# Attention weights turned by VectorE and a DRAM buffer, with a new order of units and a constant FFN pace

## The chip, the cores and the metric

The kernel runs on one core of one Trainium2 chip. The metric is the device time of one execution in microseconds (us); a quoted time is the median of a kernel's runs. In the profile of the kernel before, TensorE does the matrix products (9120 instructions), VectorE, ScalarE and GpSimd the other arithmetic (1650, 1185 and 1047), and SyncE issues the transfers (DMA) but for those of the output. "Clock" is the share of full speed that was granted to TensorE; in the 26 records of the trace before it is either 1 or one half.

## The reference

Attention with a threshold, on 8 batches of 8 heads (576 rows, head dimension 64), then a bilinear FFN over all 4608 rows. The three FFN weights come as float64 and are converted in the kernel.

```python
def _attn_ref(q, k, v, tau):                      # q, k, v: (8, 8, 576, 64)
    scale = 1.0 / np.sqrt(q.shape[-1])
    scores = scale * np.matmul(q, k.transpose(0, 1, 3, 2))
    thresh = np.max(scores, axis=-1, keepdims=True) - tau
    scores = np.where(scores >= thresh, scores, -1000000000.0)
    scores = scores - np.max(scores, axis=-1, keepdims=True)
    attn = np.exp(scores)
    attn = attn / (np.sum(attn, axis=-1, keepdims=True) + 1e-09)
    return np.matmul(attn, v).astype(np.float32)

def _moe_ref(x, w_a, w_b, w_out):                 # 512 -> 1536 -> 512
    return ((x @ w_a) * (x @ w_b) @ w_out).astype(np.float32)
```

## The kernel before

Two heads form a **pair**; there are 32. A pair has five **units**: four of 128 rows for each of its two heads (u = 0 to 3), and one with the last 64 rows of both (u = 4, the tail). A unit's scores go into two PSUM tiles (`sc`, two buffers), so the next unit's scores can start only when VectorE's mask has read these. Two units give a **half** (256 rows). Once the four pairs of a batch have delivered the same half, a block of 256 rows of FFN input `x` is complete.

```python
    def scores(i, u):
        ...
        sc = [ps_sc.tile([P, S], FP32, tag="sc", name="sc") for _ in range(n)]   # ps_sc: 2 buffers
        for c0, c1 in ((0, MAIN), (MAIN, S)):          # 512 columns, then 64
            for j in range(n):                         # the two heads: rows 0-63 and 64-127 of qT and kT
                ...
                    nc.tensor.matmul(sc[j][:, c0:c1], qT[r, u * P:(u + 1) * P],
                                     kT[r, c0:c1], start=True, stop=True)
        ...                                            # row maxima on VectorE, bias and threshold on GpSimd

    def weigh(i, u):
        ...
            nc.scalar.activation(w, s, AF.Exp, bias=bias[:, j:j + 1], scale=e_scale[:, 0:1])
        ...
            nc.vector.scalar_tensor_tensor(            # the mask; last reader of the PSUM tile
                out=ws[j], in0=s, scalar=thr[:, j:j + 1], in1=ws[j],
                op0=ALU.is_ge, op1=ALU.mult, accum_out=sums[:, j:j + 1])
        ...
        for j, w in enumerate(ws):
            nc.gpsimd.tensor_scalar(w, w, rcp[:, j:j + 1], None, op0=ALU.mult)
        weights[i, u] = ws

    def turn_pe(i, u):                                 # the weights must be turned for the product with v
        ...
                for s in range(4):
                    c = TAIL * j + s * P
                    nc.tensor.transpose(tp[:, s, :], w[:, c:c + P], ident)
                nc.scalar.copy(view[:, 5 * j:5 * j + 4], tp.rearrange("p s (i e) -> p s i e", e=Q))
        ...
```

FFN matmuls are strewn between the units: `advance(cols)` emits so many columns of them, at a `rate` set anew for each batch from what is waiting.

```python
    units = [(i, u) for i in range(NPR) for u in range(NT + 1)]
    ...
    for g in range(len(units) + PV_LAG):               # PV_LAG = 1
        if g < len(units):
            ...
            scores(i, u)
            ...
        if before is not None:
            turn(*before)                              # the unit before this one
        ...
            weigh(i, u)
            for _ in range(2):
                convert_weights()                      # float64 -> float32, a piece at a time
                load_weights(1)
        ...
        advance(rate)
        for what in due(g):
            weighted(*what)                            # product with v of a finished half
            if what[1] == 1 and what[0] % HP == HP - 1:
                rate = backlog() / (2 * UB)
        advance(rate)
```

## Time and profile before

| | before |
|---|---|
| time, median (lowest to highest of 4 runs) | 1920.09 us (1918.99 to 1921.74) |
| TensorE busy / mean clock | 1799.5 us of 1917.2 / 0.959 |
| VectorE, ScalarE, GpSimd busy | 711.5, 559.0, 808.2 us |

The page's picture of the span in 40 slices of 48 us gives the busy share of an engine in tenths (9 is 90% or more), and the granted clock likewise.

```profile
PE   4665868999999999999999999999999999999999
...
PEclk9666789999999999999999999999999999999999
```

TensorE is idle for more than a third of the first six slices and slowed in five of them, then full. The table of waits (who waited for what: us in total, times, longest) says what holds it there:

```profile
PE tp L287 <- POOL w L262: 51.1, 33, 4.3
PE sc L229 <- DVE w L255: 30.9, 9, 5.8
```

The largest wait is a turn that waits for GpSimd's scaling of the weights. The second, only nine times, is a score tile that waits for VectorE's mask to free a PSUM slot.

### The profile page before, as it was taken

What the parts mean: (1) busy time and instruction counts of PE and PEld (TensorE: products, weight loads), DVE (VectorE), ACT (ScalarE), POOL (GpSimd) and SP (SyncE); (2) the same over time, 40 slices, a digit from 0 to 9 for tenths busy, and PEclk for the clock granted to TensorE, in tenths of its full rate; (3) what the DMA queues carried; (4) which work ended last, traced back from release to release, by engine and by line L of the source; (5) the groups of instructions that cost most, each with busy time, mean ns of one, the idle gap of its engine ahead of it and who ended that gap; (6) DMA issues with size and microseconds to landing.
All of it is one profiled execution on the core that took longest, in us unless ns stands there. A gap on an engine that the chain in (4) does not pass through costs nothing.

```text
span 1917.2 us, 24375 instructions
## 1 busy us (share of the span) xinstructions
PE 1799.5 (94%) x9120; PEld 1219.7 (64%) x9120; DVE 711.5 (37%) x1650; ACT 559.0 (29%) x1185; POOL 808.2 (42%) x1047
## 2 busy tenths in 40 slices
PE   4665868999999999999999999999999999999999
PEld 2333545676757575757576767676757575758766
DVE  4666565343334333434333332332334333331000
ACT  2333322333333332333332222222323332331000
POOL 5788777434444344444444323323444344440000
PEclk9666789999999999999999999999999999999999
DMA  4223232111110111111111011001110100000000
GB/s 106 65 64 89 74 96 58 30 19 30 19 30 15 28 20 30 20 30 20 22 21 25 19 25 18 24 13 30 20 30 17 27 13 18 1 12 1 11 11 11
DMA packets 201157, 58.20 MB, mean 30 GB/s; under 512 B 191824, under 2 KB 191824, under 8 KB 201040
## 3 DMA queue, kind: packets, MB, share of 16 engines
q1 hardware_dynamic: 195792, 47.21, 11.6%
q10 hardware_dynamic: 5248, 9.44, 1.4%
q8 instruction: 72, 1.18, 0.2%
q14 instruction: 45, 0.37, 0.1%
HBM read 47.19 MB, written 9.44 MB: 30 GB/s over the span
## 4 chain that ended last, share of the span: by engine, by line
PE 84%; POOL 9%; DVE 4%; issue 2%; ACT 1%; SPq 0%; DMA 0%; POOLq 0%; DVEq 0%; ACTq 0%
PE pab L388 39%; PE po L404 20%; PE sc L229 7%; PE pv L358 6%; PE tp L287 6%; POOL w L262 4%; PE tp L293 2%; POOL low L170 2%; POOL low L169 2%; PE sc L232 2%; PE pv L355 1%; DVE w L255 1%; POOL bias L240 1%; POOL top L162 1%; DVE mx L239 1%
## 5 line engine op out<-in xcount | busy, mean ns | idle before, releaser
L262 POOL TENSOR_SCALAR w<-w,rcp 128x576 f32<-128x576 f32 x288 | 505.9, 1767 | 360.0 <-DVE rcp L260 354.0
L239 DVE TENSOR_REDUCE mx<-sc 128x1 f32<-128x576 f32 x288 | 207.3, 752 | 528.4 <-PE sc L229 458.2
L388 PE MATMUL pab<-xT,wb_sb 128*128 128x256 f32 x1536 | 389.8, 389 | 4.5 <-ACT wT L288 3.2
L404 PE MATMUL po<-wo_sb,h 128*128 128x512 f32 x864 | 389.5, 599 | 0.0
L388 PE MATMUL pab<-xT,wa_sb 128*128 128x256 f32 x1536 | 380.0, 387 | 7.2 <-ACT wT L294 7.2
L388 PEld LDWEIGHTS pab<-xT,wa_sb 128*128 128x128 f32 x1536 | 288.4, 191 | 66.0 <-issue 21.0
L388 PEld LDWEIGHTS pab<-xT,wb_sb 128*128 128x128 f32 x1536 | 287.6, 192 | 55.9 <-issue 10.5
L240 POOL TENSOR_SCALAR bias<-mx,e_nscale 128x1 f32<-128x1 f32 x288 | 95.2, 331 | 472.0 <-DVE mx L239 298.2
L255 DVE SCALAR_TENSOR_TENSOR w<-sc,thr,w 128x576 f32<-128x576 f32 x288 | 226.7, 815 | 142.0 <-ACT w L252 137.9
L404 PEld LDWEIGHTS po<-wo_sb,h 128*128 128x128 f32 x864 | 159.3, 190 | 184.0 <-issue 183.0
L288 ACT COPY wT<-tp 128x512 f32<-128x512 f32 x256 | 138.9, 588 | 415.6 <-PE tp L287 409.0
L252 ACT ACTIVATE w<-sc,bias,e_scale 128x576 f32<-128x576 f32 x288 | 230.3, 846 | 72.8 <-POOL bias L240 72.0
L398 DVE TENSOR_TENSOR h<-a,pab 128x256 f32<-128x256 f32 x216 | 90.6, 420 | 405.7 <-PE pab L388 405.3
L229 PE MATMUL sc<-kT,qT 64*128 64x512 f32 (+1 forms) x1024 | 200.8, 474 | 39.1 <-DVE w L255 30.9
L229 PEld LDWEIGHTS sc<-kT,qT 64*128 64x128 f32 x1024 | 105.9, 198 | 163.6 <-issue 153.3
L287 PE MATMUL tp<-ident,w 128*128 128x128 f32 x1024 | 152.5, 291 | 51.2 <-POOL w L262 51.1
L395 ACT COPY a<-pab 128x256 f32<-128x256 f32 x216 | 80.7, 374 | 364.0 <-PE pab L388 363.9
L287 PEld LDWEIGHTS tp<-ident,w 128*128 128x128 f32 x1024 | 116.9, 148 | 67.1 <-POOL w L262 61.3
L358 PE MATMUL pv<-wT,vm 128*64 128x256 f32 x1024 | 132.7, 404 | 0.0
L358 PEld LDWEIGHTS pv<-wT,vm 128*64 128x64 f32 x1024 | 71.3, 144 | 54.6 <-issue 29.2
L241 POOL TENSOR_SCALAR thr<-mx,cut 128x1 f32<-128x1 f32 x288 | 85.8, 298 | 0.0
L363 ACT COPY xT<-pv 128x256 f32<-128x256 f32 x64 | 23.8, 372 | 199.1 <-PE pv L358 186.6
(55 smaller groups left out, 990.4 us busy)
## 6 DMA issues: line engine op xcount, KB each, us to landing
qm<-in_q_dram SPq DMA_DIRECT2D x128, 72.0 KB, 2.4
km<-in_k_dram SPq DMA_DIRECT2D x128, 72.0 KB, 2.5
vm<-in_v_dram SPq DMA_DIRECT2D x64, 128.0 KB, 2.5
out_dram<-osb ACTq DMA_DIRECT2D x32, 256.0 KB, 2.0
raw<-in_moe_w_a_dram SPq DMA_DIRECT2D x12, 512.0 KB, 3.8
raw<-in_moe_w_b_dram SPq DMA_DIRECT2D x12, 512.0 KB, 3.8
raw<-in_moe_w_out_dram SPq DMA_DIRECT2D x12, 512.0 KB, 3.7
v_diag<-in_v_dram SPq DMA_DIRECT2D x64, 16.0 KB, 2.0
```

What stands on the lines that cost most here:

```text
L229: nc.tensor.matmul(sc[j][:, c0:c1], qT[r, u * P:(u + 1) * P], kT[r, c0:c1], start=True, stop=True)
L239: nc.vector.tensor_reduce(mx[:, c], sc[j], axis=AX.X, op=ALU.max)
L240: nc.gpsimd.tensor_scalar(bias[:, c], mx[:, c], e_nscale[:, 0:1], None, op0=ALU.mult)
L252: nc.scalar.activation(w, s, AF.Exp, bias=bias[:, j:j + 1], scale=e_scale[:, 0:1])
L255: nc.vector.scalar_tensor_tensor(out=ws[j], in0=s, scalar=thr[:, j:j + 1], in1=ws[j], op0=ALU.is_ge, op1=ALU.mult, accum_out=sums[:, j:j + 1])
L262: nc.gpsimd.tensor_scalar(w, w, rcp[:, j:j + 1], None, op0=ALU.mult)
L287: nc.tensor.transpose(tp[:, s, :], w[:, c:c + P], ident)
L288: nc.scalar.copy(view[:, 5 * j:5 * j + 4], tp.rearrange("p s (i e) -> p s i e", e=Q))
L358: nc.tensor.matmul(pv[j * D:(j + 1) * D], vm[:, j, s, :], wT[:, 5 * j + s, :], start=False, stop=(s == 3))
L388: nc.tensor.matmul(p, w[:, c, fs], xT[:, c, :], start=(c == 0), stop=(c == HP - 1))
L398: nc.vector.tensor_tensor(hid, a, pab[1], op=ALU.mult)
L404: nc.tensor.matmul(po, hs[F][:, u * P:(u + 1) * P], wo_sb[:, F, :], start=(F == 0), stop=(F == NF - 1))
```

## The change

The intent is to take the turns off TensorE, which is the bound. The kernel has VectorE turn the weights in blocks of 32x32 (256 turns of 128x576); the blocks themselves are then put in the partitions that the product with v reads by four stores to a DRAM buffer and one load of it. The product with v comes two units after a half's last unit instead of one. GpSimd gives the scaling of the weights to ScalarE, and the conversion of the FFN weights needs fewer operations. Units run in a new order, the first halves of four pairs and then their rest, so that the first FFN block is complete after 8 units. FFN runs at a constant pace. The diff, cut to its core:

```diff
-PV_LAG = 1
-WT_BUFS = 3
+PV_LAG = 2
+WT_BUFS = 2
+FFN_PACE = 0.09
...
+    scratch = pool("scratch", 3, space=bass.MemoryType.DRAM)
...                                        # convert_weights
-        nc.scalar.activation(low, lo, AF.Copy, bias=0.0, scale=2.0 ** -52)
-        nc.vector.tensor_scalar(top_u, hi, 0x7FFFFFFF, None, op0=ALU.bitwise_and)
+        nc.scalar.activation(top, hi.bitcast(FP32), AF.Abs)
+        nc.scalar.activation(low, lo, AF.Copy, bias=2.0 ** 23, scale=2.0 ** -29)
...
-        nc.gpsimd.tensor_tensor(low, low, t, op=ALU.mult)
-        nc.gpsimd.tensor_tensor(low, low, top, op=ALU.add)
...
+        nc.gpsimd.tensor_tensor(dst.bitcast(U32), top_u, low_u, op=ALU.add)
...                                        # turn
         for j, w in enumerate(ws):
-            nc.gpsimd.tensor_scalar(w, w, rcp[:, j:j + 1], None, op0=ALU.mult)
+            nc.scalar.activation(w, w, AF.Copy, scale=rcp[:, j:j + 1])
...                                        # turn_pe is gone; the VectorE turn of w into tb was there, unused
+            swap = scratch.tile([2 * NB, Q, G, W], FP32, tag="swap", name="swap")
+            for g in range(G):
+                nc.sync.dma_start(swap[:, :, g, :].rearrange("c p w -> p c w"),
+                                  tb[g * Q:(g + 1) * Q])
+            wT = work.tile([P, NSLOT, n], FP32, tag="wT", bufs=WT_BUFS, name="wT")
...
+        nc.sync.dma_start(wT, swap.rearrange("(s r) p g w -> (r p) s (g w)", r=G))
...
-    units = [(i, u) for i in range(NPR) for u in range(NT + 1)]
+    units = []
+    for i in range(0, NPR, HP):
+        units += [(p, u) for p in range(i, i + HP) for u in (0, 1)]
+        units += [(p, u) for p in range(i, i + HP) for u in (2, 3, 4)]
...
+                if g == max(first[p] - 4, 0):
+                    load_pair(p)
...
-        advance(rate)
+        advance(0.85 * PACE)
         for what in due(g):
             weighted(*what)
-            if what[1] == 1 and what[0] % HP == HP - 1:
-                rate = backlog() / (2 * UB)
-        advance(rate)
+        advance(0.15 * PACE)
```

More of the change, by code (lines that the diff above doesn't have):

```diff
@@ L20, in float_of @@
     return struct.unpack("<f", struct.pack("<I", bits))[0]
-DMA_FROM = 32
-PV_LAG = 1
-WT_BUFS = 3
+PV_LAG = 2
 XT_BUFS = 4
 W_BUFS = 4
+WT_BUFS = 2
+H_BUFS = 13
+FFN_PACE = 0.09
 @with_exitstack
@@ L76 @@
     HALF = MAIN // 2
+    GT = HALF // TAIL
     NSLOT = 9
-    GT = HALF // TAIL
+    G = P // Q
     SCALE = 1.0 / math.sqrt(D)
@@ L96 @@
     loaded = {}
-    NVD = 3
+    NVD = HP
     v_diag = [const.tile([P, 2, D], FP32, name=f"v_diag{i}") for i in range(NVD)]
@@ L110, in load_pair @@
             tiles[name] = t
-        vm = loads.tile([P, 2, NT, D], FP32, tag="vm", bufs=3, name="vm")
+        vm = loads.tile([P, 2, NT, D], FP32, tag="vm", bufs=HP, name="vm")
         vd = v_diag[i % NVD]
@@ L156, in convert_weights @@
         top = work.tile([P, CW], FP32, tag="osb", bufs=4, name="top")
-        t = work.tile([P, CW], FP32, tag="osb", bufs=4, name="t")
         low = work.tile([P, CW], FP32, tag="osb", bufs=4, name="low")
-        top_u, t_u = top.bitcast(U32), t.bitcast(U32)
-        nc.scalar.activation(low, lo, AF.Copy, bias=0.0, scale=2.0 ** -52)
-        nc.vector.tensor_scalar(top_u, hi, 0x7FFFFFFF, None, op0=ALU.bitwise_and)
-        nc.gpsimd.tensor_scalar(top, top, float_of(0x47F00000), float_of(0x38000000),
+        top_u, low_u = top.bitcast(U32), low.bitcast(U32)
+        nc.scalar.activation(top, hi.bitcast(FP32), AF.Abs)
+        nc.scalar.activation(low, lo, AF.Copy, bias=2.0 ** 23, scale=2.0 ** -29)
+        nc.gpsimd.tensor_scalar(top, top, float_of(0x47EFFFFF), float_of(0x38000000),
                                 op0=ALU.min, op1=ALU.max)
-        nc.vector.tensor_scalar(t_u, top_u, 3, 0x3FFFFFFF,
+        nc.scalar.activation(low_u, low, AF.Copy, bias=-(2.0 ** 23), scale=1.0)
+        nc.vector.tensor_scalar(top_u, top_u, 3, 0x3FFFFFFF,
                                 op0=ALU.logical_shift_left, op1=ALU.bitwise_and)
-        nc.vector.scalar_tensor_tensor(out=top_u, in0=top_u, scalar=0x40000000, in1=t_u,
+        nc.vector.scalar_tensor_tensor(out=top_u, in0=hi, scalar=0xC0000000, in1=top_u,
                                        op0=ALU.bitwise_and, op1=ALU.bitwise_or)
-        nc.vector.tensor_scalar(t_u, top_u, 0x7F800000, None, op0=ALU.bitwise_and)
-        nc.gpsimd.tensor_tensor(low, low, t, op=ALU.mult)
-        nc.gpsimd.tensor_tensor(low, low, top, op=ALU.add)
-        nc.vector.scalar_tensor_tensor(out=dst.bitcast(U32), in0=hi, scalar=0x80000000,
-                                       in1=low.bitcast(U32),
-                                       op0=ALU.bitwise_and, op1=ALU.bitwise_or)
+        nc.gpsimd.tensor_tensor(dst.bitcast(U32), top_u, low_u, op=ALU.add)
     for t in v_diag:
@@ L181 @@
     load_weights(2)
-    ident = const.tile([P, P], FP32, name="ident")
-    make_identity(nc, ident)
-    q_diag = [const.tile([P, P], FP32, name=f"q_diag{i}") for i in range(2)]
+    q_diag = [const.tile([P, P], FP32, name=f"q_diag{i}") for i in range(1)]
     for t in q_diag:
@@ L210, in prep, with prep_tail @@
         t = loaded[i]
-        qT = work.tile([P, S], FP32, tag="qT", name="qT")
-        kT = work.tile([P, S], FP32, tag="kT", name="kT")
+        qT = work.tile([P, S], FP32, tag="qT", bufs=HP, name="qT")
+        kT = work.tile([P, S], FP32, tag="kT", bufs=HP, name="kT")
         nc.vector.transpose(qT, t["q"].rearrange("p n e -> p (n e)"))
         nc.vector.transpose(kT, t["k"].rearrange("p n e -> p (n e)"))
-        qd = q_diag[i % 2]
+        prepared[i] = (qT, kT)
+    def prep_tail(i):
+        qT, qd = prepared[i][0], q_diag[0]
         for j in range(2):
@@ L218, in prep @@
             nc.gpsimd.tensor_copy(qd[r, j * TAIL:(j + 1) * TAIL], qT[r, MAIN:S])
-        prepared[i] = (qT, kT, qd)
     def scores(i, u):
-        qT, kT, qd = prepared[i]
+        qT, kT = prepared[i]
+        qd = q_diag[0]
         n = 2 if u < NT else 1
@@ L260, in weigh, with turn @@
         nc.vector.reciprocal(rcp[:, 0:n], sums[:, 0:n])
+        weights[i, u] = (ws, rcp)
+    def turn(i, u):
+        ws, rcp = weights.pop((i, u))
         for j, w in enumerate(ws):
-            nc.gpsimd.tensor_scalar(w, w, rcp[:, j:j + 1], None, op0=ALU.mult)
-        weights[i, u] = ws
-    def turned_tile(i, u):
-        h = u // 2
-        if (i, h) not in turned:
-            if u < NT:
-                turned[i, h] = work.tile([P, NSLOT, HALF], FP32, tag="wT", bufs=WT_BUFS, name="wT")
-            else:
-                turned[i, h] = work.tile([P, NSLOT, TAIL], FP32, tag="wTt", bufs=2, name="wTt")
-        return turned[i, h]
@@ L275, in turn_pe @@
-    def turn_pe(i, u):
-        ws = weights.pop((i, u))
-        wT = turned_tile(i, u)
-        if u < NT:
-            view = wT.rearrange("p s (i t e) -> p s i t e", i=4, e=Q)[:, :, :, u % 2, :]
-            tp = ps_1.tile([P, 4, P], FP32, tag="ps1", name="tp")
-            for j, w in enumerate(ws):
-                if j == 1:
-                    tp = ps_1.tile([P, 4, P], FP32, tag="ps1", name="tp")
-                for s in range(4):
-                    c = TAIL * j + s * P
-                    nc.tensor.transpose(tp[:, s, :], w[:, c:c + P], ident)
-                nc.scalar.copy(view[:, 5 * j:5 * j + 4], tp.rearrange("p s (i e) -> p s i e", e=Q))
-            tp = ps_1.tile([P, P], FP32, tag="ps1", name="tp")
-            for j, w in enumerate(ws):
-                r = slice(TAIL * j, TAIL * (j + 1))
-                c = MAIN * (1 - j)
-                nc.tensor.matmul(tp[r], w[:, c:c + TAIL], ident, start=True, stop=True)
-            nc.scalar.copy(view[:, 4], tp.rearrange("p (i e) -> p i e", e=Q))
-        else:
-            w = ws[0]
-            tps = []
-            for j in range(2):
-                r = slice(TAIL * j, TAIL * (j + 1))
-                tp = ps_1.tile([P, 4, TAIL], FP32, tag="ps1", name="tp")
-                for s in range(4):
-                    c = TAIL * j + s * P
-                    nc.tensor.transpose(tp[:, s, :], w[r, c:c + P], ident[r, r])
-                tps.append(tp)
-            tp = ps_1.tile([P, P], FP32, tag="ps1", name="tp")
-            for j in range(2):
-                r = slice(TAIL * j, TAIL * (j + 1))
-                c = MAIN * (1 - j)
-                nc.tensor.matmul(tp[r], w[:, c:c + TAIL], ident, start=True, stop=True)
-            for j in range(2):
-                nc.scalar.copy(wT[:, 5 * j:5 * j + 4], tps[j])
-                r = slice(TAIL * j, TAIL * (j + 1))
-                nc.scalar.copy(wT[r, 4], tp[r, r])
@@ L315, in turn_dma @@
-    def turn_dma(i, u):
-        ws = weights.pop((i, u))
-        wT = turned_tile(i, u)
+            nc.scalar.activation(w, w, AF.Copy, scale=rcp[:, j:j + 1])
         if u < NT:
@@ L329, in turn_dma @@
                 return
-            src = tb.rearrange("p (s r) e -> p s r e", r=4)
-            for g in range(4):
-                for r in range(4):
-                    nc.sync.dma_start(
-                        wT[r * Q:(r + 1) * Q, :, g * 2 * Q:(g + 1) * 2 * Q],
-                        src[g * Q:(g + 1) * Q, :, r, :])
+            n, W = HALF, 2 * Q
+            swap = scratch.tile([2 * NB, Q, G, W], FP32, tag="swap", name="swap")
[3 more added lines that the diff above has]
+            wT = work.tile([P, NSLOT, n], FP32, tag="wT", bufs=WT_BUFS, name="wT")
         else:
+            n = TAIL
             tb = work.tile([P, NB, Q], FP32, tag="tbt", bufs=2, name="tbt")
             nc.vector.transpose(tb.rearrange("p n e -> p (n e)"), ws[0])
-            for g in range(4):
-                j = g // 2
-                for r in range(4):
-                    s = [s for s in range(NSLOT) if 0 <= 4 * s + r - j * NB < NB]
-                    b0 = 4 * s[0] + r - j * NB
-                    nc.sync.dma_start(
-                        wT[r * Q:(r + 1) * Q, s[0]:s[-1] + 1, (g % 2) * Q:(g % 2 + 1) * Q],
-                        tb[g * Q:(g + 1) * Q, b0:b0 + 4 * len(s) - 3:4, :])
+            swap = scratch.tile([2 * NB, Q, 2, Q], FP32, tag="swapt", name="swapt")
+            for g in range(G):
+                c = slice(g // 2 * NB, (g // 2 + 1) * NB)
+                nc.sync.dma_start(swap[c, :, g % 2, :].rearrange("c p w -> p c w"),
+                                  tb[g * Q:(g + 1) * Q])
+            wT = work.tile([P, NSLOT, n], FP32, tag="wTt", bufs=1, name="wTt")
+        nc.sync.dma_start(wT, swap.rearrange("(s r) p g w -> (r p) s (g w)", r=G))
+        turned[i, u // 2] = wT
     def weighted(i, h):
@@ L396, in ffn @@
                     yield HALF
-            hid = work.tile([P, HALF], FP32, tag="h", bufs=NF + 2, name="h")
+            hid = work.tile([P, HALF], FP32, tag="h", bufs=H_BUFS, name="h")
             nc.vector.tensor_tensor(hid, a, pab[1], op=ALU.mult)
@@ L438, in backlog @@
         return len(blocks) * BLOCK_COLS + (running["left"] if running["ffn"] is not None else 0)
-    units = [(i, u) for i in range(NPR) for u in range(NT + 1)]
-    UB = HP * (NT + 1)
-    def turn(i, u):
-        (turn_dma if i >= DMA_FROM else turn_pe)(i, u)
+    units = []
+    for i in range(0, NPR, HP):
+        units += [(p, u) for p in range(i, i + HP) for u in (0, 1)]
+        units += [(p, u) for p in range(i, i + HP) for u in (2, 3, 4)]
+    first = {i: g for g, (i, u) in enumerate(units) if u == 0}
+    PACE = FFN_PACE * BLOCK_COLS
     def due(g):
         got = []
-        for d, first, last in ((PV_LAG, 1, 1), (PV_LAG, 3, 3), (PV_LAG, 4, 4)):
-            if g - d >= 0 and units[g - d][1] == last:
-                got.append((units[g - d][0], last // 2))
+        if g - PV_LAG >= 0:
+            i, u = units[g - PV_LAG]
+            if u in (1, 3, 4):
+                got.append((i, u // 2))
         return got
@@ L456 @@
     before = None
-    rate = 0.0
     for g in range(len(units) + PV_LAG):
@@ L460 @@
             i, u = units[g]
-            if u == 0 and i + 1 < NPR:
-                load_pair(i + 1)
+            for p in range(1, NPR):
+                if g == max(first[p] - 4, 0):
+                    load_pair(p)
             scores(i, u)
-            if u == 3 and i + 1 < NPR:
-                prep(i + 1)
+            for p in range(1, NPR):
+                if g == first[p] - 1:
+                    prep(p)
+            if u == 3:
+                prep_tail(i)
         if before is not None:
```

## The prediction

> **What bounds the kernel now.** I read the table of windows first, because the page's shares are averages over stages with different limits. Its columns are busy time and instruction count of each engine, granted TensorE clock, DMA share, GB/s.
>
> ```profile
> 0.00:284.00 284.00, 179.25 (x798) 107.07 (x798) 168.70 (x351) 89.47 (x167) 212.96 (x244) 0.74 0.33 81
> 284.00:1604.00 1320.00, 1311.63 (x6948) 896.35 (x6950) 486.40 (x1163) 412.30 (x890) 545.17 (x739) 1.00 0.12 25
> 1604.00:1800.00 196.00, 196.00 (x952) 135.46 (x949) 47.58 (x116) 47.05 (x105) 50.06 (x66) 1.00 0.02 9
> 1800.00:1917.00 117.00, 112.67 (x428) 80.80 (x426) 8.83 (x21) 10.15 (x25) 0.00 (x0) 1.00 0.03 10
> ```
>
> There are two regimes. From 284 us on TensorE is busy 1620 of 1633 us at full clock, so only less TensorE work shortens it. Before that GpSimd is the busiest engine (213 of 284), TensorE waits for it at clock 0.74, and no FFN runs: the first FFN input is complete only after the first four pairs, 20 units, hence 14.2 us a unit.
>
> Busy times of matmuls are modelled and overlap, so I took their cost from start to next start in the TensorE timeline of the steady part:
>
> ```profile
> 1003.64 1.19 PE L232 MATMUL sc<-kT,q_diag 128*128 128x512 f32 x4
> 1004.67 1.04 PE L287 MATMUL tp<-ident,w 128*128 128x128 f32 x8
> 1005.64 0.44 PE L293 MATMUL tp<-ident,w 128*64 128x128 f32 x4
> 1006.01 1.99 PE L388 MATMUL pab<-xT,wa_sb 128*128 128x256 f32 x8
> 1007.84 1.89 PE L388 MATMUL pab<-xT,wb_sb 128*128 128x256 f32 x8
> 1009.57 0.59 PE L355 MATMUL pv<-wT,v_diag 128*128 128x256 f32 x2
> 1010.09 1.95 PE L358 MATMUL pv<-wT,vm 128*64 128x256 f32 x16
> ...
> 1015.19 1.30 PE L229 MATMUL sc<-kT,qT 64*128 64x512 f32 x8
> 1016.32 0.46 PE L303 MATMUL tp<-ident,w 64*128 64x64 f32 x8
> 1016.71 0.44 PE L309 MATMUL tp<-ident,w 128*64 128x128 f32 x4
> 1017.08 0.70 PE L388 MATMUL pab<-xT,wb_sb 128*128 128x256 f32 x2
> ```
>
> Eight pab records take 1.73 us (1007.84 to 1009.57). The turn of a full unit takes 1.34 (1004.67 to 1006.01), of a tail unit 0.76; scores 1.13 (tail 1.03); weighted sum of a half 2.40 (1009.57 to 1011.97 by the next line), of a tail 0.87 (1020.21 to 1021.08). The chain of waits has 14 po records in 6.21 us. Over the kernel: pab 3456/8 x 1.73 = 747; po 864 x 6.21/14 = 383; scores 128 x 1.13 + 32 x 1.03 = 178; weighted sums 64 x 2.40 + 32 x 0.87 = 182; **turns 128 x 1.34 + 32 x 0.76 = 196**. Sum 1686 us. Check: 1620 lie after 284 us, so 66 lie before, and 20 units of attention alone (2.25 + 1.22 us each) are 69. The start therefore loses about 215 us.
>
> [...] one 2.1 us gap at 292.7 us is followed by eight pab records in 2.98 us instead of 1.73. [...] The trace has such a turn of 128x576 at 768 ns. [...] The trace has no store below 2 KB[...]. [...]
>
> **The change part by part.**
>
> TensorE loses all turns: 1686 - 196 = **1490 us** of work left. ScalarE loses the copies of turned tiles (139 + 36 + 21 + 13 = 209 us) and gets the scaling of the weights from GpSimd, 288 x about 0.8 us = 230 (the exp on the same shape takes 846 ns): even. GpSimd loses 506 us. VectorE gains 288 turns x 0.77 = 221 us, so some 5.5 us a unit: not the bound.
>
> Start: ten units instead of twenty run without FFN (eight units, and two of lag). In a converting unit GpSimd now has 4 x 0.31 + 2 x (0.63 + about 1.3) = 5.1 us, ScalarE 2 x 0.85 + 2 x 0.8 + 6 x 0.67 = 7.3, VectorE about 7.9 (two reductions 1.5, two masks 1.6, two turns 1.5, small ones 0.5, two conversions 2.3, q and k 0.5 on average). Before, GpSimd had 11.2 us of work in units of 14.2; the same ratio gives 10 us a unit, 100 us for ten, of which 10 x 2.25 is TensorE work: **75 us lost instead of 215**.
>
> Pace: 0.09 of a block of 62.8 us (1130/18) is 5.65 us of FFN a unit. A block lasts 11 units and the second is ready 11 after the first, so FFN does not run dry. About 150 x 0.09 = 13.6 blocks are done inside; 4.4 are left for the end, 276 us of pure TensorE work, already in the 1490.
>
> New round trip: a half is 4 stores of 1152 packets of 256 B, then one load of 1152 packets of 1 KB. For the packets:
>
> ```profile
> 757.00:758.00 1.00, 1.00 (x3) 0.38 (x2) 0.80 (x2) 0.09 (x1) 0.00 (x0) 1.00 0.72 118
> 758.00:759.00 1.00, 1.00 (x4) 0.45 (x3) 0.34 (x4) 0.00 (x0) 0.50 (x1) 1.00 0.81 130
> 759.00:760.00 1.00, 1.00 (x6) 0.43 (x6) 0.00 (x0) 0.44 (x1) 1.00 (x1) 1.00 0.31 48
> q10 hardware_dynamic: 5248, 9.44, 1.4%
> qm<-in_q_dram SPq DMA_DIRECT2D x128, 72.0 KB, 2.4
> ```
>
> These three microseconds hold one q tile, 2304 packets of 128 B, issued from 756.15: (0.72 + 0.81 + 0.31) x 16 / 2304 = 12.8 ns a packet on an engine, the first about 1.0 us after issue, landing some 0.6 us after the last. Stores of 2 KB took 1.4% x 1917 x 16 / 5248 = 82 ns, rising to about 90 without the small ones. Interpolated: 256 B 18 ns, 1 KB 47 ns. Stores: 1.0 + 4608 x 18/16 + 0.6 = 6.8; load: 1.0 + 1152 x 47/16 + 0.6 = 5.0; with semaphores **12 us** (estimate).
>
> What hides it: in the iteration after the unit, stores can start after scores (1.13), two reductions (1.6) and two turns (1.55): 4.35 us in. That iteration lasts 1.13 + 5.65 = 6.8; the next has 1.13 + 0.85 x 5.65 = 5.9 before the weighted sum. Hidden: 6.8 - 4.35 + 5.9 = 8.4 us among first halves, about 9.2 among the rest (the tail unit has one reduction). So TensorE stops 3.6 or 2.8 us per half; for the 52 halves outside the start **about 170 us**.
>
> Queue: the stores share SyncE's queue with the loads of q and k, which have three buffers. The table of waits shows it standing there already, harmlessly:
>
> ```profile
> SPq L109 <- DVE qT L213: 645.4, 24, 33.6
> ```
>
> In the new order the loads of the third and fourth pair of a group stand ahead of stores and wait for a turn of q one unit later. From the order of issues the group's stores are late by about 3, 9 and 10 us, 22 us in each of 7 later groups, 154 in all. Some of that overlaps stops counted above; I take half, **77 us**. Stops of 3 us cool the clock: [...] I take **35**[...].
>
> Sum: 1490 + 75 + 170 + 77 + 35 = 1847, say **1850 us**.
>
> **Rivals.** (a) The round trip is hidden: the two fractions of pace around the weighted sum and a lag of two look made for it, and TensorE stays the bound: 1490 + 75 + some 50 = about 1620. Against it: 12 us do not fit into 8.4, and even 1.18 MB each way at twice the seen packet rate would barely fit. (b) The wait replaces the removed work: full queue stops and full clock loss give 1490 + 75 + 170 + 154 + 94 = 1983, slower by 3%. For it: each part is visible in the program's order, and the start of the old trace shows how waits cool the clock. [...] (c) VectorE or ScalarE becomes the bound: 5.5 and about 4 us of a 7.9 us unit speak against it outside the start.
>
> **Range and chances.** Both regimes are open, so the range is wide: 1690 (half the stops) to 1990 (all of b). Faster by over 2% means below 1882: that needs the stops to stay under 320 us, which my middle sum does with 280. A kernel so finely set (pace, fractions, buffers) was probably kept because it gained, which lifts faster to 0.56; same 0.20; slower 0.24.
>
> **What would show it.** Right: no tp matmuls; TensorE nearly full before about 110 us; in the middle TensorE's largest wait is pv for the DMA of wT, 3 to 4 us most times, over 10 once in 20 units; SyncE waits for its own stores; clock under 1.00 there; last 276 us at full TensorE. Median landing of the load near 5 us, of each store 3 to 6. Wrong: no pv wait and full TensorE from 110 us on (case a), or landings of 10 us and more with TensorE under 75% busy, or VectorE as the releaser of most waits.

## More of the kernel before

The framework that builds the program chooses each engine's order of instructions itself, by its own estimate of when each becomes ready.

## The result and the profile after

The changed kernel takes **2289.18 us** (2287.38 to 2291.16, 4 runs): 1.192 times the time before (95% interval 1.190 to 1.194). Here and below a ratio is the mean time of one kernel's runs over the mean of the other's in the same rounds, so it isn't quite the ratio of the medians quoted. The prediction's range ended at 1990.

The same picture, now in slices of 57 us:

```profile
PE   3578678797788877887879777987788778999999
...
PEclk9768777797789877987779877887788778999999
```

The plateau is gone. TensorE sits between 70 and 90% in most slices, and the clock with it, until the last six. The table of windows shows the same in numbers (busy us and count of TensorE, weight loads, VectorE, ScalarE and GpSimd; then clock, DMA share, GB/s):

```profile
0.00:110.00 110.00, 45.91 (x124) 21.96 (x124) 72.87 (x145) 58.35 (x88) 43.17 (x85) 0.88 0.68 178
110.00:2000.00 1890.00, 1535.95 (x5990) 988.09 (x5991) 763.62 (x1635) 540.20 (x883) 201.42 (x636) 0.82 0.46 109
2000.00:2287.00 287.00, 281.50 (x1087) 201.52 (x1086) 21.49 (x51) 25.48 (x63) 0.00 (x0) 1.00 0.03 10
```

The start is short and the pure-FFN end is full, as predicted. Everything is lost in the 1890 us between, where no engine is full: VectorE is busy 40% of them, ScalarE 29%. TensorE's largest waits:

```profile
PE sc L233 <- DVE w L259: 332.0, 92, 6.7
PE sc L236 <- DVE w L259: 34.6, 11, 4.7
PE sc L233 <- DVE kT L214: 31.8, 5, 8.2
PE pv L308 <- DMA wT<-swap: 10.6, 2, 7.1
```

The transfer that the prediction looked at costs 10.6 us. The nine waits for a mask, 30.9 us, have become 92 with 332 us, and 103 with 367 us if those of the tail units (second row) are counted. A piece of TensorE's timeline (start, duration, what, and idle time before it with its releaser) shows one group of them:

```profile
1144.38 1.19 PE L236 MATMUL sc<-kT,q_diag 128*128 128x512 f32 x4
1145.50 1.29 PE L233 MATMUL sc<-kT,qT 64*128 64x512 f32 x4
1151.11 3.10 PE L233 MATMUL sc<-kT,qT 64*128 64x512 f32 x8 [4.32 <-DVE w L259]
1156.59 2.36 PE L233 MATMUL sc<-kT,qT 64*128 64x512 f32 x4 [2.38 <-DVE w L259]
...
1160.03 3.33 PE L311 MATMUL pv<-wT,vm 128*64 128x256 f32 x16
```

Scores of one unit follow scores of another with no FFN between them. Both PSUM slots are then full, and TensorE stands still through the chain of maximum, bias, exp and mask, here 4.32 and 2.38 us. Eight score records after such a stop take 3.10 us where the prediction's fence has 1.30, and the products with v take 3.33 instead of 1.95: the clock's records stand at one half from 1149.2 to 1162.9 us. A shorter stop, 2.25 us from 446.27 us, was followed by half clock too, from 449.5 to 456.3 us. Some 65 us before the stops of the fence, from 1077.66 us, 48 FFN matmuls ran in one piece of 20.87 us. That FFN was meant to fill these stops.

VectorE's timeline shows what it did in the longer of these stops (1146.79 to 1151.11 us):

```profile
1146.83 0.76 DVE L243 TENSOR_REDUCE mx<-sc 128x1 f32<-128x576 f32 x1 [0.46 <-PE sc L233]
1147.50 2.75 DVE L277 STREAM_TRANSPOSE tb<-w 128x576 f32<-128x576 f32 x4
1150.17 0.78 DVE L259 SCALAR_TENSOR_TENSOR w<-sc,thr,w 128x576 f32<-128x576 f32 x1
```

Between maximum and mask it turned the weights of earlier units, the new work of this change. Laid over all 103 stops for a mask, 367 us, VectorE was busy for 306 us of them: 116 with turns (in 39 of the stops), 110 with maxima, 108 with masks. So no engine is full on average, but in the stops VectorE nearly is.

To size this in every run I laid the clock's records over TensorE's busy time. "Loss to the half clock" is half of the busy time that lies in stretches of half clock; what is left of the busy time is its work at full clock (an estimate: it takes work at half clock to last twice as long; in the trace after, `pab` matmuls started 216 ns apart, median of 2199, where the record is 1, and 427 ns, median of 63, where it is one half). The three columns add up to the span.

| us | work at full clock | idle | loss to the half clock | span |
|---|---|---|---|---|
| before | 1747 | 118 | 53 | 1917 |
| after | 1587 | 423 | 277 | 2286 |

The change took 160 us of work off TensorE and put 305 us of idle time and 224 us of slow clock in its place.

### The profile page after: what moved, and what is told of

It reads as the page before. It is cut to its first block, busy times and chain, and to the rows that moved or that the text cites. A ratio compares the mean times of both kernels' runs of the same rounds, so it can differ in the third digit from the quotient of the medians.

```text
span 2286.4 us, 20952 instructions
## 1 busy us (share of the span) xinstructions
PE 1863.4 (81%) x7200; PEld 1211.6 (53%) x7200; DVE 858.0 (38%) x1830; ACT 624.0 (27%) x1033; POOL 244.6 (11%) x721
## 4 chain that ended last, share of the span: by engine, by line
PE 74%; DVE 12%; issue 4%; ACT 3%; DMA 3%; SPq 2%; POOL 1%; DVEq 0%; POOLq 0%; ACTq 0%
PE pab L341 32%; PE po L357 16%; PE sc L233 11%; PE pv L311 9%; DVE w L259 4%; DVE tb L277 4%; PE pv L308 3%; DVE mx L243 2%; PE sc L236 2%; ACT w L256 2%; DMA swap<-tb 1%; POOL bias L244 1%; ACT w L271 1%; DMA out_dram<-osb 1%; SPq L115 1%
## 5 line engine op out<-in xcount | busy, mean ns | idle before, releaser
L233 PE MATMUL sc<-kT,qT 64*128 64x512 f32 (+1 forms) x1024 | 355.2, 615 | 363.8 <-DVE w L259 332.0
L233 PEld LDWEIGHTS sc<-kT,qT 64*128 64x128 f32 x1024 | 184.6, 257 | 519.3 <-issue 507.4
L341 PE MATMUL pab<-xT,wb_sb 128*128 128x256 f32 x1536 | 375.4, 388 | 0.0
L271 ACT ACTIVATE w<-w,rcp 128x576 f32<-128x576 f32 x288 | 209.3, 767 | 199.1 <-DVE rcp L264 198.6
L311 PE MATMUL pv<-wT,vm 128*64 128x256 f32 x1024 | 202.8, 566 | 0.0
L277 DVE STREAM_TRANSPOSE tb<-w 128x576 f32<-128x576 f32 x256 | 176.4, 745 | 6.1 <-ACT w L271 3.3
L311 PEld LDWEIGHTS pv<-wT,vm 128*64 128x64 f32 x1024 | 100.9, 206 | 103.1 <-issue 95.5
L361 ACT COPY osb<-po 128x512 f32<-128x512 f32 x36 | 21.1, 586 | 350.3 <-PE po L357 350.3
L236 PE MATMUL sc<-kT,q_diag 128*128 128x64 f32 (+1 forms) x128 | 55.9, 563 | 34.6 <-DVE w L259 34.6
L308 PE MATMUL pv<-wT,v_diag 128*128 128x256 f32 x128 | 73.0, 672 | 10.6 <-DMA wT<-swap 10.6
```

What stands on the lines that cost most here:

```text
L233: nc.tensor.matmul(sc[j][:, c0:c1], qT[r, u * P:(u + 1) * P], kT[r, c0:c1], start=True, stop=True)
L236: nc.tensor.matmul(sc[j][:, c0:c1], qd, kT[:, c0:c1], start=True, stop=True)
L271: nc.scalar.activation(w, w, AF.Copy, scale=rcp[:, j:j + 1])
L277: nc.vector.transpose(tb[:, j * NB:(j + 1) * NB, (u % 2) * Q:(u % 2 + 1) * Q], w.rearrange("p (n e) -> p n e", e=Q))
L308: nc.tensor.matmul(pv, vd.rearrange("p j d -> p (j d)"), wT[:, 4, :], start=True, stop=False)
L311: nc.tensor.matmul(pv[j * D:(j + 1) * D], vm[:, j, s, :], wT[:, 5 * j + s, :], start=False, stop=(s == 3))
```

## The experiments

All twelve were correct. The first question was whether the order in which TensorE gets its instructions does this (my theory after seeing the traces) or what the text does (a lag that is too short, the transfers, the pace). The control for every experiment is the kernel before, in the same rounds.

### TensorE in the order of the text

```diff
-                    nc.tensor.matmul(sc[j][:, c0:c1], ...)
+                    tc.keep_in_program_order(nc.tensor.matmul(sc[j][:, c0:c1], ...))
```

and the same around every other matmul of the changed kernel. Nothing else in the text differs.

> The changed kernel with TensorE's instructions kept in the order of the program text (scores, 0.85 of the pace, weighted sum, 0.15, scores); nothing else is touched. In the built order of the changed kernel 220 of 288 score tiles follow another with no FFN between; pinned it is 138, with at most 6.2 us of FFN in one run. Theory A (the order in which the build put TensorE's instructions is the cause): the 367 us of waits of scores for the masks fall under 120 us, stops move to the weighted sum waiting for wT (the prediction's 3 to 4 us each), clock above 0.90, time 1800 to 2000 us. Theory B (the round trip through DRAM holds TensorE back in whatever order): 2200 us or more, now with wT as the releaser.

**2001.28 us**, ratio 1.041 (1.038 to 1.044), clock 0.919 in the profiled run; expected were 1800 to 2000. So 288 of the 369 us lost against before went with the pin on TensorE. It isn't TensorE's order alone that differs: when the two programs are built again, most instructions of VectorE and ScalarE have other places too. The built orders can be compared without the chip. In the changed kernel, 220 of the 288 score tiles follow the tile before them with no FFN in between, and the longest run of FFN between two score tiles is 34.8 us of work. In the order of the text it is 138 tiles (128 of them the second head of the same unit) and 6.2 us; in the kernel before, 149 and 10.0. An excerpt of the built order of the changed kernel:

```
912 L236 Matmult sc<-kT,q_diag_107 128x512
913 L236 Matmult sc<-kT,q_diag_107 128x64
914 L233 Matmult sc<-kT,qT 128x512
915 L233 Matmult sc<-kT,qT 128x64
...
920 L233 Matmult sc<-kT,qT 128x512
921 L233 Matmult sc<-kT,qT 128x64
922 L308 Matmult pv<-wT,v_diag_78 128x256
923 L311 Matmult pv<-wT,vm 64x256 x8
924 L341 Matmult pab<-xT,wa_sb 128x256 x4
```

Three units stand together, five score tiles for two slots. There is a second flaw: a unit's two heads don't always run next to each other, as they do in the text. Next to each other, the two cost no more time than one: in the timeline above, four records of one head take 1.29 us at full clock (at 1145.50 us), and in the prediction's fence eight records of two heads 1.30. In the changed kernel 55 of 128 units lose this, 36 because TensorE stops for a PSUM slot between the heads and 19 because other matmuls stand there; in the order of the text none.

What remains in this run is what the prediction had expected, in TensorE's waits:

```profile
PE pv L308 <- DMA wT<-swap: 227.0, 42, 24.1
```

but 17 of TensorE's stops at the turned weights are over 8 us long. SyncE's timeline shows why (the count is of issues; the last of them waits for what it needs):

```profile
804.09 4.36 SPq L285 DMA_DIRECT2D swap<-tb  x4
...
814.09 0.38 SPq L298 DMA_DIRECT2D wT<-swap  x1
...
891.58 14.20 SPq L285 DMA_DIRECT2D swap<-tb  x5
905.97 0.47 SPq L298 DMA_DIRECT2D wT<-swap  x1
```

Normally the load follows 10 us after its first store. At 891.58 a fifth store, the first of the *next* half, stands ahead of the load, and the load comes after 14.4 us. That is so at 15 of the 64 loads, and 15 of the 17 long stops are theirs. SyncE's order is built too (in the changed kernel 28 loads stand so, but there TensorE was late itself and hardly waited for them).

### SyncE in the order of the text as well

```diff
+    every nc.sync.dma_start also wrapped in tc.keep_in_program_order
```

> The changed kernel with TensorE's and SyncE's instructions both in the order of the program text (with TensorE alone it took 2001 us; there the build puts the next half's first store ahead of the load of a half, and the load waits up to 14 us behind it). If that order of SyncE makes the long stops of the weighted sum (42 stops, 227 us, longest 24), they shrink to 3 to 4 us each: 1880 to 1940 us. If the q and k loads, which stand ahead of stores in the text, make them: 1980 us or more.

**1847.41 us**, ratio 0.961 (0.960 to 0.963), better than both branches of the expectation. Another 154 us, and the kernel is now faster than before. Its largest wait:

```profile
PE pv L308 <- DMA wT<-swap: 153.9, 38, 21.3
```

This is the program that the prediction had reasoned about, and its 1850 lies 3 us off; the last section but one shows how much of that is luck.

### The control: pinning the kernel before

```diff
+    every TensorE instruction of the kernel before wrapped in tc.keep_in_program_order
```

> Control: the kernel before with TensorE's instructions pinned to the order of the program text. Its built order is nearly that already (148 against 149 tiles with no FFN before), so 1920 us within 1%; more would mean that pinning itself costs.

**1936.8 us**, ratio 1.008 (1.006 to 1.010). Pinning is no gain of its own; before, the built order was slightly better than the text's.

### The changed text, untouched, under another estimate

The build can estimate durations in a second way, which gives another order. Not a line of the kernel proper changes:

```diff
-    with _tile.TileContext(nc) as tc:
+    with _tile.TileContext(nc, schedule_with_timeline_sim=True) as tc:
```

> The changed kernel, its text untouched, built with the build's other estimate of instruction times; this alone gives another order: 96 of 288 score tiles with no FFN before (220 as it was), longest run of FFN 12 us (35). Theory A: 1850 to 2020 us, score waits under 120 us. If bunching is a symptom and not the cause: 2200 us or more.

**1850.56 us**, ratio 0.964 (0.961 to 0.966), clock 0.960. The same text at 1850 and at 2289 us: the built order (of all engines together) is the cause, not something that the pins do by the way. Waits for the mask are down from 332 us:

```profile
PE sc L233 <- DVE w L259: 47.4, 16, 7.1
```

In this order 68 of 128 units have their heads apart. At full clock a head alone took 1.22 us from its start to that of the next matmul (99 cases), and the two heads of a unit next to each other took 1.23 together, interleaved (24 cases) or one after the other (16). So what counts is that nothing stands between them, and 68 x 1.22 is some 83 us (an estimate). The work at full clock is 1635 us against 1545 of the text's order, some 90 us; its idle time and clock loss, 150 and 59 us, are lower than those of the text's order (234 and 66).

### The turn alone undone

```diff
 the changed kernel, with turn_pe, turned_tile and ident of before;
 ScalarE's scaling, the conversion, the unit order and the pace stay
```

> The changed kernel with the turn alone undone: TensorE turns the weights into PSUM, ScalarE copies them, no DRAM buffer; unit order, pace, conversion, ScalarE's scaling stay as changed. Its built order has 137 of 288 score tiles with no FFN before. If the turn (its order or its transfers) is the cause: 1490 + 196 of TensorE work and 75 to 110 us of start, so 1750 to 1810 us, clock above 0.96. If the unit order or the constant pace is the cause: above 2000 us.

**1809.73 us**, ratio 0.942 (0.941 to 0.944), clock 0.981. With the turn back on TensorE, the rest of the change gains 110 us with no pin at all, and the built order has 6.2 us and 137 tiles, where the text's had 6.2 and 138. So the turn is what makes the build bunch the instructions.

### The turn alone done

```diff
 the kernel before, with the changed turn (VectorE blocks, DRAM buffer), ScalarE's scaling, PV_LAG 2, WT_BUFS 2
```

> The kernel before with the turn alone changed (VectorE blocks, DRAM buffer, ScalarE's scaling, lag 2, two wT buffers); unit order, rate and conversion of before. Its built order is bunched as in the changed kernel (233 of 288). Theory A: scores wait for masks as in the changed kernel, 2200 to 2450 us (the long start of before comes on top). If the bunching only hurts together with the new unit order: about 1900.

**2418.76 us** (one round; ratio 1.259), clock 0.812. Its built order: 233 tiles, longest FFN run 35.1 us. Its largest wait is the same one:

```profile
PE sc L228 <- DVE w L254: 357.3, 98, 23.9
```

The two runs bracket the cause: with the turn through DRAM and the order of the build's first estimate the kernel is slow under either unit order, and without it fast under the new one.

### A longer lag, with the order free

The rival said that the lag of two units was too short, and TensorE was idle for that reason.

```diff
-PV_LAG = 2
+PV_LAG = 3
+    NVD = HP + 1; vm with HP + 1 buffers; tbt with 1, a with 2 (to make room)
```

> As a_lag3_sp, but in the order that the build chooses. 210 of 288 score tiles have no FFN before them, runs of FFN up to 26 us. Theory A: the lag does not help, scores wait for masks: 2150 to 2350 us. If the lag alone cures it: under 1800 us.

**2254.54 us** (one round; ratio 1.174): 35 us better than the changed kernel, no cure. The wait for the mask stays:

```profile
PE sc L233 <- DVE w L259: 315.6, 92, 5.5
```

### The same lag, in the order of the text

```diff
 the kernel above, with TensorE and SyncE in the order of the text
```

> Both queues in the order of the text and the weighted sum one unit later (lag 3; five v tiles, one tbt, two a tiles to make room). The round trip takes some 16 us (stores 10, load 6.4) and gets 7 to 9 us more cover, 15.5 to 18. If the waiting for the round trip is all that is left: stops for wT under 80 us, clock above 0.95, 1600 to 1720 us. If transfers or the one queue can't deliver a half in time at this pace: above 1850 us.

**1775.99 us**, ratio 0.925 (0.923 to 0.926). Here the lag is worth 71 us against 1847, between the two branches of the expectation (1600 to 1720, above 1850). The stops at the turned weights, over TensorE's timeline after the first 110 us (some carry another releaser in the table of waits), go from 50 with 159 us to 21 with 98.

### Loads of a pair one unit later, in the order of the text

The prediction had charged 77 us to loads of q and k that stand ahead of stores in SyncE's queue and wait for a free buffer. Issuing them one unit later takes that wait away.

```diff
-                if g == max(first[p] - 4, 0):
+                if g == max(first[p] - 3, 0):
```

> As a_pin_sp (both queues in the order of the text, 1847 us), with the loads of q, k and v issued three units ahead instead of four. Then the third and fourth pair of a group no longer stand ahead of a half's stores while they wait for a buffer. The prediction put 154 us on that, and took half, 77. If the loads at the head of the queue cost that: 1690 to 1790 us, the longest stop of the weighted sum under 12 us (21 now). If they cost nothing: 1830 to 1860 us.

**1842.0 us**, ratio 0.960 (0.956 to 0.963): 5 us, within the spread of its own four runs (1834.4 to 1850.4). The stops were 55 with 150 us. The queue cost next to nothing here.

### Both

```diff
 the kernel above
-PV_LAG = 2
+PV_LAG = 3                 # no further buffers
```

> As a_look3, with the weighted sum one unit later (lag 3; with the later loads no further buffers are needed). Round trip 16 us, cover 15.5 to 18. If waiting was all that the transfers cost: stops for wT under 40 us, 1600 to 1700 us, below every kernel so far (a_lag3_sp 1776). If the queue can't keep up: 1750 us or more.

**1752.89 us** (1748.1 to 1755.5), ratio 0.912 (0.911 to 0.914). This beats both kernels, 167 us below before and 536 below after, but not by as much as hoped: the time falls in the expectation's second branch, while the waits for the turned weights (30.9 us) fit its first. With one more unit of lag and a free queue, only 16 stops with 50 us are left at the turned weights. The largest wait is now for the turned k. It was 16.3 us with the later load alone and 23.7 with the longer lag alone; why both together raise it was not looked into:

```profile
PE sc L233 <- DVE kT L214: 69.1, 18, 14.3
PE pv L308 <- DMA wT<-swap: 30.9, 11, 5.9
```

### The new unit order and the pace alone

```diff
 the turn-undone kernel above, with the conversion and the GpSimd scaling of before
```

> The new order of units and the constant pace alone: TensorE's turn, GpSimd's scaling and the conversion of before (lag 2 and the buffers of the changed kernel). With the new conversion and ScalarE's scaling it was 1810 us (a_tp), the kernel before 1920. If the order gives the shorter start: 1800 to 1850 us. If GpSimd's conversion and scaling bind the start whatever the order: 1870 us or more.

**1922.71 us**, ratio 1.001 (0.999 to 1.002). The new order alone gains nothing.

### The conversion and the scaling alone

```diff
 the kernel before, with the changed conversion and ScalarE's scaling
```

> The kernel before with the new conversion and ScalarE's scaling alone; TensorE's turn, the old order of units and its rate. a_order (the order alone) took 1922 us, a_tp (both) 1810. If the conversion and the scaling alone shorten the start: 1800 to 1850 us, the first 20 units in some 200 us instead of 284. If it takes the new order as well: 1870 us or more.

**1858.98 us**, ratio 0.968 (0.966 to 0.969), between the two branches of the expectation. GpSimd's relief alone is worth 61 us. The first 284 us of the three kernels say why the two parts don't simply add; first the unit order alone, then the relief alone, then both (the turn-undone kernel):

```profile
0.00:284.00 284.00, 174.89 (x741) 108.58 (x741) 160.31 (x326) 77.05 (x145) 193.84 (x215) 0.75 0.34 85
```

```profile
0.00:284.00 284.00, 228.44 (x1033) 139.27 (x1034) 145.26 (x313) 175.68 (x325) 105.82 (x199) 0.78 0.37 93
```

```profile
0.00:284.00 284.00, 239.96 (x1224) 158.94 (x1225) 160.28 (x329) 182.91 (x338) 107.11 (x197) 0.88 0.39 97
```

In the first, GpSimd (fifth engine) is still the busiest, 194 of 284 us, as it was before with 213; TensorE got 175 us, no more than before's 179. Only when GpSimd falls to 107 does the earlier FFN start find room. Then it is worth 49 us more (1858.98 less 1809.73).

## Why the prediction was wrong

The terms of its sum, beside the kernel in the order of the text (TensorE and SyncE pinned) and the kernel as it ran:

| us | predicted | order of the text | after |
|---|---|---|---|
| TensorE work at full clock | 1490 | 1545 | 1587 |
| stops in the start (first 110 us) | 75 | 71 | 64 |
| stops later | 170 + 77 | 164 | 359 |
| loss to the half clock | 35 | 66 | 277 |
| sum | 1847 | 1846 | 2286 |

**The step that failed is the one the part "What hides it" stands on.** It says "in the iteration after the unit, stores can start after scores (1.13), two reductions (1.6) and two turns (1.55): 4.35 us in. That iteration lasts 1.13 + 5.65 = 6.8". That takes the program's text for the order in which TensorE and SyncE get their work: one unit's scores, then 5.65 us of FFN. The order that ran was built, not written, and it had no FFN between many units. Three terms follow from that. The clock is the largest: 277 us, not 35 ("Stops of 3 us cool the clock"; the 35, and the 94 in rival (b), were estimates of mine that no trace showed). The waits are next: 359 us after the start, not 247, and for the mask, not for the transfer. The heads that no longer run side by side add about 42 us to the work (1587 against 1545). The rivals missed it as well. Rival (b) had "full queue stops and full clock loss" at 1983; rival (c) looked for an engine that is full, and none is. No rival asked whether a chain of short dependent steps, with no engine full over a unit, could set the pace once nothing stood between its links. One of its signs of being wrong did come true, "VectorE as the releaser of most waits": 398 of TensorE's 423 idle us.

The profile of before held only a hint. Its waits for the mask all lie in the first 210 us, where no FFN stands between units: they show what happens when the filler is missing. I read them as a trait of the start.

**Removed work: right; its level was not.** TensorE's work at full clock fell from 1747 us to 1545 in the order of the text, 202; predicted 196. The level was 55 too low. For the kernel before it was 61 too low (1686), and the check that seemed to confirm it agreed by luck: it put 66 us of work before 284 us, and 133 lie there. The first FFN matmul ran at 224.7 us, after 21 units (so 10.7 us a unit, not 14.2), and by 284 us 24 units' scores and 112 FFN records had run, some 105 us at the prediction's own spacings (an estimate). The rest, 28 us there and 33 after it, no run explains.

**Start: near in size, wrong in its reason.** 71 and 64 us idle against 75; with the clock's share, 88 and 92 us were lost when FFN began, at 120 and 142 us where 100 was predicted. The start of before was misread with the same 284: it had lost 130 us when its FFN began, not 215. And the step "ten units instead of twenty" doesn't gain by itself: the order alone gave nothing, the relief of GpSimd 61 us, both 110.

**Round trip: near.** Predicted 12 us; in the run with TensorE pinned, 10 us from the first store to the load's issue and 6.2 us to its landing, some 16. The packets took about what was interpolated. From the queues' rows (packets, MB, share of 16 engines), before and then after:

```profile
q1 hardware_dynamic: 195792, 47.21, 11.6%
```

```profile
q1 hardware_dynamic: 682704, 217.11, 40.3%
```

The trace keeps each packet's size and time. The 331,776 packets of 256 B that were added (294,912 of them stored) took 18.1 ns each on an engine, predicted 18; the 73,728 of 1 KB took 53 on average (median 46), predicted 47. A byte cost 1.36 times as much in the small packets as in those of 1 KB. What lengthens the trip is the issue: the four stores at 804.09 us took SyncE 0.31, 0.61, 1.54 and 1.76 us, 4.36 in all, a time that the prediction had not counted. (A slip in its part "What hides it": 1.13, 1.6 and 1.55 make 4.28, not 4.35.)

**Stops at the transfer: right in kind, and nearly in size.** 52 stops and 170 us were predicted; in the order of the text there were 50 with 159 us. One more unit of lag takes most of them away.

**Queue: wrong.** 77 us predicted, 5 measured, within the spread. The 1850 of the text's order is thus partly luck: work 55 and clock 31 too low, stops 87 too high.

**Open.** The runs show that the turn through DRAM makes the build's first estimate bunch the scores and that its second doesn't, not which estimated duration does it. The interplay of the stop lengths and the clock was measured only as a whole: no run changed the stops without changing their number. No run moved VectorE's turns out of the way of the masks alone, so their share of the loss isn't shown.

## What to carry to other kernels

A gain computed from the text of a program holds only if the engines get their instructions in that order: compare the built order with the text before you reckon what hides behind what, above all when a change adds a long transfer. Look for chains of short steps on several engines with only two buffers between them. Here the filler between the links kept TensorE and its clock up (clock 0.948 in the run of 1847 us, 0.842 in that of 2289); without it this kernel lost 700 of 2286 us (423 idle, 277 to the clock), though no engine was full over the stretch. Pin the order of the engines that the schedule depends on, then tune lag and look-ahead: 2289 us became 1847, and then 1753.
